# Weight loads ahead of the activations in one queue, and the first two chunks made block by block with plain products

## The chip, the cores and the metric

One core of one Trainium2 chip. The metric is the device time of one execution in microseconds (us). Each kernel ran several times. "Span" is the profiled execution seen from inside, some 2 us shorter than the device time of that same execution.

## The reference

x is fp32, 8 x 3008 x 256; the weights are float64, w_in 256 x 2048 and w_out 2048 x 256; the result is fp32.

```python
X = np.fft.fft(x, axis=1)
X = np.fft.fft(X, axis=2)
attn = X.real.astype(np.float32)                 # (8, 3008, 256)
h = attn.reshape(8 * 3008, 256) @ w_in           # inner dimension 2048
g = np.maximum(0.01 * h, h)
out = (g @ w_out).astype(np.float32)
```

## The kernel before

The transform along 256 is folded into w_in: a product of w_in with a small table gives `wf` ("fold"). The transform along 3008 is a product with sine and cosine tables ("dft"), made for 16 units (a batch element, even or odd frequencies). The result is worked off in 48 chunks of 2 x 251 or 2 x 250 columns, three to a unit, and for each chunk in 8 blocks `f` of the inner dimension: 384 steps. A step has an "up" (four products, VectorE's additions, ScalarE's leaky ReLU) and, three steps later, a "down" into w_out. VectorE's additions also use two rows: `wn`, a row of the folded weights, and `nb`, made from one column of x (`nyx`) by a transform of 8 rows ("nyquist"). Both go out to DRAM and come back in another layout. "Down" is a fast scheme with seven products in place of eight. It needs four sums of the activations in every step and four combinations of w_out's tiles; both are GpSimd's work.

```python
    def up(j, f):
        ...                                       # 4 products, then VectorE makes cos and g
        nc.scalar.activation(g, g, ACT.Lrelu)                                    # line 394
        a = [[g[:, r, h * n : (h + 1) * n] for h in range(2)] for r in range(2)]
        s = work.tile([P, 4, CW], F32, tag="s", bufs=4, name="s")
        s1, s2, s3, s4 = (s[:, i, 0:n] for i in range(4))
        nc.gpsimd.tensor_tensor(s1, a[1][0], a[1][1], op=ALU.add)
        nc.gpsimd.tensor_tensor(s2, s1, a[0][0], op=ALU.subtract)
        nc.gpsimd.tensor_tensor(s3, a[0][0], a[1][0], op=ALU.subtract)
        nc.gpsimd.tensor_tensor(s4, a[0][1], s2, op=ALU.subtract)
        hidden[j, f] = a[0][0], a[0][1], s4, a[1][1], s1, s2, s3

    turns = (0, 1, 5, 6, 4, 2, 3)

    def down(j, f):
        ...                                       # sums[j]: seven sums in four PSUM banks
        for i, p in enumerate(turns):             # seven products, line 416
            nc.tensor.matmul(sums[j][p], lhsT=still[p], rhs=moving[p], ...)
        ...                                       # after the last block: 7 additions, store
```

The weights arrive as float64 words. VectorE turns each 128x512 tile into fp32 with five instructions (and ScalarE with two): two on integers in `begin` (lines 247, 248), three in `end` (lines 260 to 262). There are 16 such tiles, eight of each weight. The head of the program:

```python
    w0 = load_w_in(0)                             # w_in, block 0: two tiles
    t0 = load_x(0, nc.scalar)                     # x: 2 x 1.5 MB on ScalarE's queue
    nc.scalar.dma_start(nyx, x_nyq)
    nc.sync.dma_start(feat_sb, ...)
    w2 = load_w_in(2 * WN)                        # w_in, block 2
    for n in range(4):
        load_tab(nc.sync, n, 0)                   # transform tables
    convert(w0)
    fold_w_in(0, w0)
    ...                                           # folds of x, then the transforms of unit 0
    convert(w2)
    fold_w_in(2 * WN, w2)
    spread_wn(0)()                                # the row wn goes through DRAM
    step(0)
    step(1)
    step(2)
    ...                                           # the other weights, one step between two of them
```

`step(at)` makes the "up" of step `at` and the "down" of step `at - 3`. The order written here is not binding inside an engine: the built program has its own fixed order, made by the scheduler.

Of the kernel before, what the change touches and what calls it, by code (L numbers as in the profile page):

```python
# [39 lines left out]
F32 = mybir.dt.float32  # L43
# [6 lines left out]
P = 128  # L50
# [7 lines left out]
CW = 251  # L58
NF = F // P
NH = NF // 2  # L60
WN = 512
WB = WN // D
# [88 lines left out]
def tile_fnet_leaky_relu(  # L151
# [24 lines left out]
    def load_x(b, q=None):  # L176
        t = xp.tile([P, 2, 2, NI * 2, D], F32, tag="x", bufs=1, name="xt")
        for h in range(2):
            (q or nc.sync).dma_start(t[:, h], x[b, :, h].rearrange("p e i r d -> p e (i r) d"))
        return t  # L180
# [3 lines left out]
    def fold_rows(t, h):  # L184


        a, z = t[:, h, 0], t[:, h, 1]
        nc.vector.tensor_tensor(a, a, z, op=ALU.add)  # L188
        lo, hi = a[:, :, 1:P], a[:, :, P + 1 : D]
        nc.vector.tensor_tensor(z[:, :, P + 1 : D], lo, hi, op=ALU.subtract)  # L190
        nc.vector.tensor_tensor(z[:, :, 1:P], lo, hi, op=ALU.add)
        nc.scalar.copy(z[:, :, 0:1], a[:, :, 0:1])
        nc.gpsimd.memset(z[:, :, P : P + 1], 0.0)
# [19 lines left out]
    def load_tab(q, n, c):  # L213
        t = const.tile([P, NI, KC], F32, name=f"tab_{n}_{c}")
        q.dma_start(t, seq_tab[n, c])
        tabs[n, c] = t
# [49 lines left out]
    def convert(made):  # L266
        for w in made:
            w.begin()
        for w in made:
            w.end()  # L270

    def load_w_in(f0):
        n, made = w_in.shape[1] // F, []
        for a in range(2):
            w = work.tile([P, WN], F32, tag="win", bufs=4, name="win")
            src = w_in[a * P : (a + 1) * P, n * f0 : n * (f0 + WN)].rearrange("p (c n) -> p c n", c=1)
            made.append(Weights(src, w))
        return made

    def fold_w_in(f0, made):  # L280

        for w in range(2):
            pt = up_ps()
            for a in range(2):
                nc.tensor.matmul(pt, lhsT=feat_sb[:, a, w * P : (w + 1) * P], rhs=made[a].dst, start=(a == 0), stop=(a == 1))  # L285
            nc.scalar.copy(wf[:, w, f0 : f0 + WN], pt)

    def spread_wn(f0):


        row = wn_dram[:, f0 : f0 + WN]
        nc.scalar.dma_start(row.rearrange("(o h) n -> o h n", o=1), wf[0:1, 1].rearrange("o (h n) -> o h n", h=2)[:, :, f0 : f0 + WN])
        at = f0 // P

        def rest():
            for h in range(2):
                nc.scalar.dma_start(wn[:, h * NH + at : h * NH + at + WN // P], row[h].rearrange("(q p) -> p q", p=P))
        return rest
# [9 lines left out]
    def combine_w_out(f):  # L308

        b = [[wo[:, h, f : f + WB, i * P : (i + 1) * P] for i in range(2)] for h in range(2)]  # L310
        t = [wt[:, i, f : f + WB, :] for i in range(4)]
        for to, x, y in ((t[0], b[0][1], b[0][0]), (t[1], b[1][1], t[0]), (t[2], b[1][1], b[0][1]), (t[3], b[1][0], t[1])):
            nc.gpsimd.tensor_tensor(to, x, y, op=ALU.subtract)
# [34 lines left out]
    def fold_nyquist():  # L348
        nc.vector.tensor_tensor(nyb, nya, nyb, op=ALU.add)
        nc.vector.tensor_tensor(nya[:, 0], nyb[:, 0], nyb[:, 1], op=ALU.add)  # L350
        nc.vector.tensor_tensor(nya[:, 1], nyb[:, 0], nyb[:, 1], op=ALU.subtract)
# [20 lines left out]
    mixed, spreads, hidden, sums = {}, {}, {}, {}  # L372
    units = [(b, c) for b in range(B) for c in range(2)]
    blocks, _ = chunks()
    steps = [(j, f) for j in range(len(blocks)) for f in range(NH)]

    def up(j, f):
        b, c, at, n, _ = blocks[j]
        pt = [up_ps("cos_ps"), up_ps("sin_ps")]
        for blk in range(2):  # L380
            for h in range(2):
                fs = slice((h * NH + f) * P, (h * NH + f + 1) * P)
                nc.tensor.matmul(pt[blk][:, h * n : (h + 1) * n], lhsT=wf[:, blk, fs],  # L383
                                 rhs=mixed[b, c][blk][:, at : at + n], start=True, stop=True)
        cos = work.tile([P, 2 * CW], F32, tag="cos", bufs=3, name="cos")
        for h in range(2):
            hs = slice(h * n, (h + 1) * n)
            nc.vector.scalar_tensor_tensor(cos[:, hs], in0=spreads[b, c][:, at : at + n],  # L388
                                           scalar=wn[:, h * NH + f : h * NH + f + 1],
                                           in1=pt[0][:, hs], op0=ALU.mult, op1=ALU.add)  # L390
        g = work.tile([P, 2 * WN], F32, tag="g", bufs=5, name="g")[:, 0 : 4 * n].rearrange("p (r k) -> p r k", r=2)
        nc.vector.tensor_tensor(g[:, 0], cos[:, 0 : 2 * n], pt[1][:, 0 : 2 * n], op=ALU.add)  # L392
        nc.vector.tensor_tensor(g[:, 1], cos[:, 0 : 2 * n], pt[1][:, 0 : 2 * n], op=ALU.subtract)  # L393
        nc.scalar.activation(g, g, ACT.Lrelu)  # L394
        a = [[g[:, r, h * n : (h + 1) * n] for h in range(2)] for r in range(2)]
        s = work.tile([P, 4, CW], F32, tag="s", bufs=4, name="s")
        s1, s2, s3, s4 = (s[:, i, 0:n] for i in range(4))
        nc.gpsimd.tensor_tensor(s1, a[1][0], a[1][1], op=ALU.add)  # L398
# [5 lines that stand above are left out]

    turns = (0, 1, 5, 6, 4, 2, 3)

    def down(j, f):
        _, _, _, n, first = blocks[j]
        if f == 0:
            banks = [ps.tile([P, 512], F32, tag="sum", bufs=4, name="sum_ps") for _ in range(4)]  # L410
            sums[j] = {p: banks[i // 2][:, 256 * (i % 2) : 256 * (i % 2) + n] for i, p in enumerate(turns)}
        moving = hidden.pop((j, f))
        still = (wo[:, 0, f, 0:P], wo[:, 1, f, 0:P], wo[:, 1, f, P:D], wt[:, 3, f], wt[:, 0, f], wt[:, 1, f], wt[:, 2, f])
        for i, p in enumerate(turns):

            nc.tensor.matmul(sums[j][p], lhsT=still[p], rhs=moving[p], start=(f == 0 and i % 2 == 0),  # L416
                             stop=(f == NH - 1), skip_group_check=True)
        if f < NH - 1:
            return
        p1, p2, p3, p4, p5, p6, p7 = (sums[j][p] for p in range(7))  # L420
        o = work.tile([P, 2 * WN], F32, tag="o", bufs=2, name="o")[:, 0 : 4 * CW].rearrange("p (a n) -> p a n", a=2)
        e = work.tile([P, 2 * WN], F32, tag="e", bufs=2, name="e")[:, 0 : 4 * CW].rearrange("p (a n) -> p a n", a=4)
        q1, u2, u3, v = (e[:, i, 0:n] for i in range(4))
        c11, c21, c12, c22 = (o[:, d, r * n : (r + 1) * n] for d in range(2) for r in range(2))
        nc.scalar.copy(q1, p1)
        for to, x, y in ((c11, q1, p2), (u2, q1, p6), (u3, u2, p7), (v, u2, p5), (c22, u3, p5), (c12, v, p3), (c21, u3, p4)):
            nc.vector.tensor_tensor(to, x, y, op=ALU.add)
        for d in range(2):
            nc.sync.dma_start(out[d * P : (d + 1) * P, first : first + 2 * n], o[:, d, 0 : 2 * n])

    lag = 3

# [24 lines left out]
    nc.vector.memset(inf[:, 0:1], 1151.0)  # L457
    nc.vector.memset(inf[:, 1:2], 255.0 * 2.0**23)
    w0 = load_w_in(0)
    t0 = load_x(0, nc.scalar)  # L460
    nc.scalar.dma_start(nyx, x_nyq)
    nc.sync.dma_start(feat_sb, feat_tab.rearrange("(a p) n -> p a n", p=P))
    w2 = load_w_in(2 * WN)
    for n in range(4):
        load_tab(nc.sync, n, 0)
    convert(w0)
    fold_w_in(0, w0)
    fold_rows(t0, 0)
    fold_rows(t0, 1)
    fold_halves(0, t0)  # L470
    fold_nyquist()
    nyquist(0)()
    dft(units[0], 0)()
    spread(units[0])
    dft(units[0], 1)()
    convert(w2)
    fold_w_in(2 * WN, w2)
    spread_wn(0)()
    step(0)
    step(1)  # L480
    step(2)
    o = load_w_out(0)
    convert(o)
    combine_w_out(0)
    w = load_w_in(WN)
    convert(w)
    fold_w_in(WN, w)
    step(3)
    w = load_w_in(3 * WN)
    for n in range(4):  # L490
        load_tab(nc.sync, n, 1)
    convert(w)
    fold_w_in(3 * WN, w)
    spread_wn(WN)()
    nyquist(1)()
    spread(units[1])
    for blk in range(2):
        dft(units[1], blk)()
    for f in range(WB, NH, WB):
        o = load_w_out(f)  # L500
        convert(o)
        combine_w_out(f)
        step(3 + f // 2)
    for at in range(7, len(steps) + lag):
        step(at)


# [28 lines left out]
```

## Time and profile before

| | before |
|---|---|
| device time, median of 6 runs | 1979.0 us (1978.8 to 1979.3) |
| span of the profiled run | 1977.1 us |
| TensorE busy | 1939.4 us |
| TensorE waiting | 33.2 us |
| first product starts | 23.0 us |
| first "up" starts | 44.5 us |

How to read it: span less busy less waiting leaves 4.5 us (nearly all of it behind the last product, which ends at 1972.6).

### The profile page before, as it was taken

The numbers are of one execution on the slowest core, as the hardware profiler recorded it, in microseconds if no ns is written. First come the engines' busy times: TensorE is split into PE (matmuls) and PEld (weight loads), VectorE is DVE, ScalarE is ACT, GpSimd is POOL, SyncE is SP. The second block draws the span as 40 slices with busy tenths as digits, with TensorE's granted clock in tenths as the row PEclk, the third lists the DMA queues.
The fourth block names the chain that finished last, engine by engine and source line by source line (L and its number), as shares of the span: only waits on it lengthen the run. The fifth ranks groups of instructions, "written<-read, shape, count | busy, mean of one in ns | idle before, by whom it ended". The sixth has DMA issues, their size and how long they took to land.

```text
span 1977.1 us, 24341 instructions
## 1 busy us (share of the span) xinstructions
PE 1939.4 (98%) x8888; PEld 1681.7 (85%) x8888; DVE 1103.0 (56%) x2089; ACT 460.7 (23%) x524; POOL 1092.1 (55%) x1572
## 2 busy tenths in 40 slices
PE   5899999999999999999999999999999999999999
PEld 2588888888888888888888888888888888888888
DVE  7965444574454745556554665447544474445444
ACT  3422222222222222222222222222222222222221
POOL 0675555565555655556555565556645565555554
PEclk9999999999999999999999999999999999999999
DMA  7300000020000100010000200002000020000000
GB/s 290 126 11 29 11 11 19 22 82 11 19 21 18 76 11 19 21 75 19 11 29 11 83 11 22 19 11 83 21 11 19 11 93 11 11 19 21 11 11 22
DMA packets 25598, 70.99 MB, mean 36 GB/s; under 512 B 4596, under 2 KB 17268, under 8 KB 23432
## 3 DMA queue, kind: packets, MB, share of 16 engines
q1 hardware_dynamic: 22928, 66.18, 9.3%
q10 hardware_dynamic: 2552, 3.26, 0.5%
q8 instruction: 71, 1.16, 0.2%
q14 instruction: 47, 0.39, 0.1%
HBM read 44.72 MB, written 24.71 MB: 35 GB/s over the span
## 4 chain that ended last, share of the span: by engine, by line
PE 96%; DVE 3%; DMA 1%; issue 0%; ACT 0%; ACTq 0%; DVEq 0%; SPq 0%
PE sum_ps L416 57%; PE sin_ps L383 16%; PE cos_ps L383 16%; PE dft_ps L318 6%; DMA raw<-in_w_in_dram 1%; DVE power L261 0%; PE up_ps L285 0%; DVE power L248 0%; DVE wo L260 0%; DVE wo L262 0%; DVE xt L188 0%; DVE wo L247 0%; DVE cos L388 0%; DMA wn<-wn_dram 0%; DVE win L260 0%
## 5 line engine op out<-in xcount | busy, mean ns | idle before, releaser
L388 DVE SCALAR_TENSOR_TENSOR cos<-nb,wn,cos_ps 128x251 f32<-128x251 f32 (+1 forms) x768 | 330.5, 472 | 725.4 <-PE cos_ps L383 724.4
L398 POOL TENSOR_TENSOR s<-g 128x251 f32<-128x251 f32 (+1 forms) x384 | 285.2, 743 | 797.1 <-ACT g L394 791.0
L394 ACT ACTIVATE g<-g 128x1004 f32<-128x1004 f32 (+1 forms) x384 | 399.1, 1039 | 1317.4 <-DVE g L393 1303.0
L416 PE MATMUL sum_ps<-s,wt 128*128 128x251 f32 (+1 forms) x2304 | 550.6, 374 | 0.0
L416 PEld LDWEIGHTS sum_ps<-s,wt 128*128 128x128 f32 x2304 | 434.1, 188 | 55.0
L383 PE MATMUL cos_ps<-mix,wf 128*128 128x251 f32 (+1 forms) x1536 | 388.8, 375 | 7.7 <-DVE cos L388 7.7
L383 PE MATMUL sin_ps<-mix,wf 128*128 128x251 f32 (+1 forms) x1536 | 388.5, 375 | 0.8 <-DVE mix L327 0.8
L416 PE MATMUL sum_ps<-g,wo 128*128 128x251 f32 (+1 forms) x1536 | 388.7, 375 | 0.0
L383 PEld LDWEIGHTS cos_ps<-mix,wf 128*128 128x128 f32 x1536 | 291.8, 190 | 43.0 <-DVE cos L388 8.1
L416 PEld LDWEIGHTS sum_ps<-g,wo 128*128 128x128 f32 x1536 | 291.8, 190 | 40.2
L383 PEld LDWEIGHTS sin_ps<-mix,wf 128*128 128x128 f32 x1536 | 290.7, 189 | 36.2 <-DVE mix L327 1.2
L399 POOL TENSOR_TENSOR s<-s,g 128x251 f32<-128x251 f32 (+1 forms) x384 | 294.0, 766 | 0.0
L401 POOL TENSOR_TENSOR s<-g,s 128x251 f32<-128x251 f32 (+1 forms) x384 | 276.4, 720 | 29.9
L392 DVE TENSOR_TENSOR g<-cos,sin_ps 128x502 f32<-128x502 f32 (+1 forms) x384 | 259.8, 676 | 49.6 <-DVE cos L388 11.2
L393 DVE TENSOR_TENSOR g<-cos,sin_ps 128x502 f32<-128x502 f32 (+1 forms) x384 | 257.1, 670 | 0.0
L400 POOL TENSOR_TENSOR s<-g 128x251 f32<-128x251 f32 (+1 forms) x384 | 255.2, 665 | 0.0
L416 PE MATMUL sum_ps<-g,wt 128*128 128x251 f32 (+1 forms) x768 | 225.2, 375 | 0.0
L416 PE MATMUL sum_ps<-s,wo 128*128 128x251 f32 (+1 forms) x768 | 225.2, 375 | 0.0
L416 PEld LDWEIGHTS sum_ps<-s,wo 128*128 128x128 f32 x768 | 145.5, 189 | 17.0
L416 PEld LDWEIGHTS sum_ps<-g,wt 128*128 128x128 f32 x768 | 145.9, 190 | 16.5
L318 PE MATMUL dft_ps<-tab,xt 128*128 128x377 f32 (+1 forms) x384 | 127.0, 480 | 1.7 <-DVE nyq L327 1.7
L318 PEld LDWEIGHTS dft_ps<-tab,xt 128*128 128x128 f32 x384 | 72.5, 189 | 45.8 <-DVE nyq L327 2.3
(43 smaller groups left out, 435.4 us busy)
## 6 DMA issues: line engine op xcount, KB each, us to landing
xt<-in_x_dram SPq DMA_DIRECT2D x14, 1536.0 KB, 10.0
out_dram<-o SPq DMA_DIRECT2D x80, 251.0 KB, 2.3
tab<-in_seq_tab_dram SPq DMA_DIRECT2D x8, 565.5 KB, 8.2
raw<-in_w_in_dram SPq DMA_DIRECT2D x8, 512.0 KB, 4.4
raw<-in_w_out_dram SPq DMA_DIRECT2D x8, 512.0 KB, 3.9
out_dram<-o SPq DMA_DIRECT2D x16, 250.0 KB, 2.4
xt<-in_x_dram ACTq DMA_DIRECT2D x2, 1536.0 KB, 10.0
nb<-nyq_dram SPq DMA_DIRECT2D x8, 376.5 KB, 4.1
```

The lines of the kernel that those rows point to most:

```text
L318: nc.tensor.matmul(ps_t[0:m, 0 : KW[c]], lhsT=z_of(i), rhs=tabs[n, c][:, i, 0 : KW[c]], start=(i == 0), stop=(i == NI - 1))
L383: nc.tensor.matmul(pt[blk][:, h * n : (h + 1) * n], lhsT=wf[:, blk, fs], rhs=mixed[b, c][blk][:, at : at + n], start=True, stop=True)
L388: nc.vector.scalar_tensor_tensor(cos[:, hs], in0=spreads[b, c][:, at : at + n], scalar=wn[:, h * NH + f : h * NH + f + 1], in1=pt[0][:, hs ...
L392: nc.vector.tensor_tensor(g[:, 0], cos[:, 0 : 2 * n], pt[1][:, 0 : 2 * n], op=ALU.add)
L393: nc.vector.tensor_tensor(g[:, 1], cos[:, 0 : 2 * n], pt[1][:, 0 : 2 * n], op=ALU.subtract)
L394: nc.scalar.activation(g, g, ACT.Lrelu)
L398: nc.gpsimd.tensor_tensor(s1, a[1][0], a[1][1], op=ALU.add)
L399: nc.gpsimd.tensor_tensor(s2, s1, a[0][0], op=ALU.subtract)
L400: nc.gpsimd.tensor_tensor(s3, a[0][0], a[1][0], op=ALU.subtract)
L401: nc.gpsimd.tensor_tensor(s4, a[0][1], s2, op=ALU.subtract)
L416: nc.tensor.matmul(sums[j][p], lhsT=still[p], rhs=moving[p], start=(f == 0 and i % 2 == 0), stop=(f == NH - 1), skip_group_check=True)
```

## The change

Its intent: w_in, needed first, is not to share the memory bandwidth with x (in `before`, between 2 and 12 us, x's queue moved 3.00 MB, in packets of 12,288 bytes, and w_in's 0.99 MB, in packets of at most 4,096); so all loads go into one queue in order of use, and both first w_in blocks are converted and folded before x is touched. Then VectorE, which has to convert the other twelve tiles during the first steps, is to be relieved: the first two chunks are made together, block by block, so that each pair of tiles serves two steps, and with eight plain products, which need neither GpSimd's sums nor the combined w_out.

```diff
-    steps = [(j, f) for j in range(len(blocks)) for f in range(NH)]
+    plain = 2
+    steps = [(j, f) for f in range(NH) for j in range(plain)]
+    steps += [(j, f) for j in range(plain, len(blocks)) for f in range(NH)]
 ...                                              # in up():
+        if j < plain:
+            hidden[j, f] = a
+            return
 ...
+    def down_plain(j, f):
+        ...                                       # two PSUM banks
+        for d in range(2):
+            for r in range(2):
+                for h in range(2):
+                    nc.tensor.matmul(sums[j][d][:, r * n : (r + 1) * n], lhsT=wo[:, h, f, d * P : (d + 1) * P], rhs=a[r][h], ...)
+        if f == NH - 1:                           # two ScalarE copies and the store
 ...                                              # the head:
     w0 = load_w_in(0)
-    t0 = load_x(0, nc.scalar)
-    nc.scalar.dma_start(nyx, x_nyq)
     nc.sync.dma_start(feat_sb, ...)
     w2 = load_w_in(2 * WN)
+    nc.sync.dma_start(nyx, x_nyq)
+    t0 = load_x(0)
     for n in range(4):
         load_tab(nc.sync, n, 0)
     convert(w0)
     fold_w_in(0, w0)
+    convert(w2)
+    fold_w_in(2 * WN, w2)
+    spread_wn(0)()
+    fold_nyquist()
     ...                                           # folds of x, then the transforms of unit 0
-    convert(w2)
-    fold_w_in(2 * WN, w2)
-    spread_wn(0)()
 ...                                              # then: one pair of weight tiles, two steps, in turn;
                                                  # unit 1's transforms come later, GpSimd's combinations last
```

More of the change, by code (lines that the diff above doesn't have):

```diff
@@ L405, in tile_fnet_leaky_relu, with put, out_tile @@
     turns = (0, 1, 5, 6, 4, 2, 3)
+    def put(o, n, first):
+        for d in range(2):
+            nc.sync.dma_start(out[d * P : (d + 1) * P, first : first + 2 * n], o[:, d, 0 : 2 * n])
+    def out_tile():
+        return work.tile([P, 2 * WN], F32, tag="o", bufs=2, name="o")[:, 0 : 4 * CW].rearrange("p (a n) -> p a n", a=2)
+    def down_plain(j, f):
+        _, _, _, n, first = blocks[j]
+        if f == 0:
+            sums[j] = [ps.tile([P, 512], F32, tag="sum", bufs=4, name="sum_ps") for _ in range(2)]
+        a = hidden.pop((j, f))
+        for d in range(2):
+            for r in range(2):
+                for h in range(2):
+                    nc.tensor.matmul(sums[j][d][:, r * n : (r + 1) * n], lhsT=wo[:, h, f, d * P : (d + 1) * P], rhs=a[r][h],
+                                     start=(f == 0 and r == 0 and h == 0), stop=(f == NH - 1 and h == 1), skip_group_check=True)
+        if f == NH - 1:
+            o = out_tile()
+            for d in range(2):
+                nc.scalar.copy(o[:, d, 0 : 2 * n], sums[j][d][:, 0 : 2 * n])
+            put(o, n, first)
     def down(j, f):
+        if j < plain:
+            down_plain(j, f)
+            return
         _, _, _, n, first = blocks[j]
@@ L420, in down @@
         p1, p2, p3, p4, p5, p6, p7 = (sums[j][p] for p in range(7))
-        o = work.tile([P, 2 * WN], F32, tag="o", bufs=2, name="o")[:, 0 : 4 * CW].rearrange("p (a n) -> p a n", a=2)
+        o = out_tile()
         e = work.tile([P, 2 * WN], F32, tag="e", bufs=2, name="e")[:, 0 : 4 * CW].rearrange("p (a n) -> p a n", a=4)
@@ L427, in down @@
             nc.vector.tensor_tensor(to, x, y, op=ALU.add)
-        for d in range(2):
-            nc.sync.dma_start(out[d * P : (d + 1) * P, first : first + 2 * n], o[:, d, 0 : 2 * n])
+        put(o, n, first)
     lag = 3
@@ L470, in tile_fnet_leaky_relu @@
     fold_halves(0, t0)
-    fold_nyquist()
     nyquist(0)()
@@ L475, in tile_fnet_leaky_relu, with some_steps @@
     dft(units[0], 1)()
-    convert(w2)
-    fold_w_in(2 * WN, w2)
-    spread_wn(0)()
-    step(0)
-    step(1)
-    step(2)
+    at = 0
+    def some_steps(n):
+        nonlocal at
+        for _ in range(n):
+            step(at)
+            at += 1
     o = load_w_out(0)
     convert(o)
-    combine_w_out(0)
+    some_steps(plain)
     w = load_w_in(WN)
@@ L487, in tile_fnet_leaky_relu @@
     fold_w_in(WN, w)
-    step(3)
+    some_steps(plain)
     w = load_w_in(3 * WN)
-    for n in range(4):
-        load_tab(nc.sync, n, 1)
     convert(w)
@@ L494, in tile_fnet_leaky_relu @@
     spread_wn(WN)()
+    some_steps(plain)
+    o = load_w_out(WB)
+    for n in range(4):
+        load_tab(nc.sync, n, 1)
+    convert(o)
+    some_steps(plain)
     nyquist(1)()
     spread(units[1])
-    for blk in range(2):
-        dft(units[1], blk)()
-    for f in range(WB, NH, WB):
+    for f in range(2 * WB, NH, WB):
         o = load_w_out(f)
         convert(o)
+        some_steps(plain)
+        dft(units[1], f // WB - 2)()
+    for f in range(0, NH, WB):
         combine_w_out(f)
-        step(3 + f // 2)
-    for at in range(7, len(steps) + lag):
-        step(at)
+    some_steps(len(steps) + lag - at)
 def kernel(x, moe_w_in, moe_w_out):
```

## The prediction

A difference of the ends of -13.9 us, taken as -13.5 after an allowance of about half a microsecond, gave 1979.0 - 13.5 = 1965.5 us.

> **What bounds the kernel now.** I read the page's first and fourth parts, then the waits of TensorE, then the timeline of TensorE and of VectorE over the first 110 us.
>
> ```profile
> PE 1939.4 (98%) x8888; PEld 1681.7 (85%) x8888; DVE 1103.0 (56%) x2089; ACT 460.7 (23%) x524; POOL 1092.1 (55%) x1572
> ...
> PE 96%; DVE 3%; DMA 1%; issue 0%; ACT 0%; ACTq 0%; DVEq 0%; SPq 0%
> ```
>
> TensorE is busy for 98% of a span of 1977.1 us and is 96% of the chain that ended last. Hardly anything but its own work and its idle time can move the end. All of its waits are these four:
>
> ```profile
> PE up_ps L285 <- DVE win L262: 23.0, 1, 23.0
> PE cos_ps L383 <- DVE cos L388: 7.7, 1, 7.7
> PE dft_ps L318 <- DVE nyq L327: 1.7, 1, 1.7
> PE sin_ps L383 <- DVE mix L327: 0.8, 1, 0.8
> ```
>
> That is 33.2 us, and the timeline puts every one of them before 86.3 us. From there to 1971.4 us TensorE never waits (busy 1884.2 of 1884.2 us between 87.2 and 1971.4). So the case is decided in the first 90 us. TensorE there:
>
> ```profile
> 23.00 6.47 PE L285 MATMUL up_ps<-win,feat_sb 128*128 128x512 f32 x8 [23.00 <-DVE win L262]
> 29.40 3.97 PE L318 MATMUL dft_ps<-tab,nyx 128*8 128x377 f32 x12
> 33.30 7.88 PE L318 MATMUL dft_ps<-tab,xt 128*128 128x377 f32 x24
> 41.02 3.60 PE L285 MATMUL up_ps<-win,feat_sb 128*128 128x512 f32 x8
> ...
> 55.76 2.04 PE L383 MATMUL cos_ps<-mix,wf 128*128 128x251 f32 x4 [7.75 <-DVE cos L388]
> ```
>
> The same eight instructions take 6.47 us when TensorE comes out of idleness and 3.60 us later: an idle spell costs about 3 us more than itself. The first 23 us are a chain, w_in arriving and VectorE converting it:
>
> ```profile
> 1.18 11.64 DMA raw<-in_w_in_dram
> 12.84 0.43 DVE win L247
> ```
>
> The second half of the first w_in block lands only at 12.84 us. The two 1.5 MB pieces of x on ScalarE's queue, issued at the same instant, land at about 8 and 13 us. After it VectorE is nearly full (8.6 to 10 of each 10 us from 20 us on): it takes in x, converts sixteen 128x512 weight tiles from float64 words (five instructions each) and makes the activations. The 7.75 us wait is for the row wn, which goes through DRAM and can start only when the second w_in block is folded, at 44 us.
>
> [...] while both queues are full, x moves about 3 MB in the time in which w_in moves 1 MB, the packets being 12,288 and 4,096 bytes, so x in its own queue holds back what is needed first. [...] full clock comes some 5.5 us after the first matmul, is lost in the 7.75 us wait (mean granted clock 0.66 between 50 and 60 us), and returns at about 59 us. [...] the 128x512 tensor_scalar of line 248 takes 0.42 us with GpSimd idle and up to 0.95 us with it busy. [...] a 251-column product, two records here, takes 0.424.
>
> **The change part by part: extra products.** In steady state a step is 4.67 us: 1.70 for four "up" products (8 records x 0.212 us) and 2.97 for the seven of the fast scheme (14 records). The plain form has eight: 16 x 0.212 = 3.40. Sixteen steps (two chunks, eight blocks) pay 0.425 each: +6.8 us of TensorE, all on the path. GpSimd loses 64 sums, VectorE fourteen additions; neither is on the path.
>
> **Head loads.** The queue carries, in order, w0 (1.05 MB), feat (0.26), w2 (1.05), nyx (0.10), x (3.15), four tables (2.32), two w_out tiles (1.05). Before, some 4.3 MB had come by 12.84 us and 390 to 430 GB/s flowed after. I take a landing as 2.8 us + MB/0.42: first w_in tiles at 4.1 and 5.3, w2 at 7.2 and 8.4, x at 12.4 and 16.1, tables from 17.5 to 21.6, w_out at 22.9 and 24.1 us.
>
> **The head, on the built order of each engine.** VectorE's spacings without GpSimd are 0.34 us for a tensor_scalar, 0.60 for each scalar_tensor_tensor (2.5 us a tile), 1.67 + 0.86 + 0.86 for half of x, 3.3 for the last two folds of x. The order now is w0, w2, x. w0 is converted at about 10 us (ScalarE's first table load, 1.28 us, delays it a little); TensorE starts at 9.7 in place of 23.0. w2 is done at 15, x's folds at 18.5, 21.9, 23.6 and 25.2. TensorE: fold w0, cold, to about 16; fold w2 to 19.7; the 8-row transform, as soon as two tables are in, to 23.6; the two transforms of the first unit to 31.6. So the first step begins at about 31.6 instead of 44.5 with both w_in blocks already folded. wn is back by about 27. The row nb: its butterfly waits for x's last fold, 26.1 us; before, nb landed 6.1 us after its butterfly, so about 32.3, just when VectorE is free for it (33.6). The 7.75 us wait goes.
>
> **The catch-up.** VectorE must still convert the four tiles of w_in blocks 1 and 3 among the first steps. Following the built order: TensorE waits about 1 us for the second transform's butterfly, 1.5 us for the first activation (at 37.2), 1.3 us for the last w_in tile of block 1 (42.8), 2.3 us for that of block 3 (52.4), and makes the sixth "up" by 60.5 us. After that two plain steps plus their pair of tiles cost VectorE 4 + 5 = 9 us, against 2 x 5.09 = 10.2 of TensorE, and GpSimd, with no sums to make, no longer slows it. I expect no further wait: the combinations (16 GpSimd operations) have four steps' time, and the four sum banks are freed by four ScalarE copies while TensorE does the next "up".
>
> **The sum.** Before, at 87.2 us, five "ups", one "down" and all transforms of unit 1 are done. After, at 60.5 us: six "ups" and two plain "downs", but the three transforms of unit 1 (36 records x 0.32 = 11.5 us) still ahead. Difference of the ends: 60.5 - 87.2 - 1.70 (one more "up") - 2.97 (one more "down") + 14 x 0.425 (plain steps still ahead) + 11.5 = -13.9 us. The check by idle time: before 33.2 us idle and about 5 of cold clock; after 9.7 + 6 idle and 3 cold; 38 - 19 - 6.8 = 12. With half a microsecond for what I overlooked: 1979.0 - 13.5 = 1965.5 us.
>
> **The rivals.** First, the weights bound VectorE however the steps are arranged, so the idle time moves into the first six steps. For it: VectorE is nearly full from 12.8 to 92 us before, and by my count is still full to 64 us after. Against it: some 30 us of its time was spent at rates slowed by GpSimd, now idle there. If the stalls came to 11 us instead of 6, the time is about 1971. Second, the single queue turns against the change: x and the tables arrive last, and w_in block 1 stands behind the write of the 8-row transform, which waits for VectorE. For it: any load behind that write is held until 26 us. Against: tables have 1 to 5 us of slack and block 1 is wanted only at 38. If the queue ran 15% slower the head would come 2 to 3 us later, about 1968. Third, the plain products eat the gain: if only the earlier start were kept and the middle wait returned in another form (nb in place of wn), 13 - 6.8 leave 6, about 1973. The nb chain has little slack in my timeline (1 us), so I give this some weight. In the other direction: if the stalls of the catch-up vanish (tiles converted earlier than I reckon) the time is about 1960.
>
> **Range and chances.** The central case is 1965.5; the rivals stand at 1968 to 1973, the good case at 1960. Stalls I have not seen are likelier than ones I invented, so the range leans up: 1961 to 1971. Two per cent is 39.6 us: more than all idle time there is (33.2), and the extra products are 6.8 against a saving that would have to turn into a loss of 33. So within 2% is as good as certain: 0.98, with 0.01 on either side.
>
> **What would show it.** First matmul near 9.7 us, first "cos" near 31.6 us, and no wait of TensorE over 3 us between the first step and 90 us; waits of TensorE summing to about 16 us in place of 33.2; line 429's products 256 x 2 records at 0.212 us apart; no wait after 65 us, and none where the third chunk takes the sum banks. VectorE's 128x512 conversions should stay near 0.42 and 0.69 us throughout. It is wrong if w_in's second half lands after 8 us, if TensorE waits on nb or on a w_out tile for more than 3 us, if the clock drops again after 31 us, or if the period of a later step differs from 4.67 us.

## The result, and the profile after

| | before | after |
|---|---|---|
| device time, median of 6 runs | 1979.0 us | 1964.85 us (1964.4 to 1966.2) |
| span of the profiled run | 1977.1 us | 1964.4 us |
| TensorE busy | 1939.4 us | 1945.9 us |
| TensorE waiting | 33.2 us | 14.0 us |
| first product / first "up" | 23.0 / 44.5 us | 10.24 / 32.65 us |

The ratio is 0.9929 (0.9917 to 0.9942), so within 2%. A ratio here and below is the mean time of one kernel's fast runs over the mean of the other's of the same rounds, so not quite the ratio of the medians. The outputs of the changed kernel, and of every experiment, agreed with the reference.

The page of the changed kernel, busy time by engine and the chain that ended last:

```profile
PE 1945.9 (99%) x8920; PEld 1687.8 (86%) x8920; DVE 1090.4 (56%) x2075; ACT 462.4 (24%) x526; POOL 1036.1 (53%) x1508
...
PE 98%; DVE 1%; DMA 1%; ACT 0%; SPq 0%; issue 0%; DVEq 0%
```

TensorE has 6.5 us more to do, and 32 records (16 products, two records each) more. VectorE and GpSimd have less. All waits of TensorE (us in total, times, longest):

```profile
PE up_ps L286 <- DVE win L263: 10.2, 1, 10.2
PE sum_ps L429 <- ACT g L397: 2.0, 1, 2.0
PE dft_ps L319 <- DVE xt L199: 1.0, 1, 1.0
PE sin_ps L386 <- DVE mix L327: 0.8, 1, 0.8
```

19.2 us of waiting have gone and 6.5 us of work have come: 12.7, the difference of the two spans. (The medians differ by 14.15: the profiled run of the changed kernel took 1966.17 us, the longest of the six; see the two kinds of runs below.) The wait for w_in has shrunk from 23.0 to 10.2 us and the middle wait of 7.7 us, for wn, is no more. TensorE's timeline (start, length, line, operation, count, idle time before and its releaser):

```profile
10.24 9.75 PE L286 MATMUL up_ps<-win,feat_sb 128*128 128x512 f32 x16 [10.24 <-DVE win L263]
19.92 3.98 PE L319 MATMUL dft_ps<-tab,nyx 128*8 128x377 f32 x12
24.93 7.88 PE L319 MATMUL dft_ps<-tab,xt 128*128 128x377 f32 x24 [1.03 <-DVE xt L199]
32.65 1.01 PE L386 MATMUL cos_ps<-mix,wf 128*128 128x251 f32 x4
...
39.26 6.20 PE L429 MATMUL sum_ps<-g,wo 128*128 128x251 f32 x20 [1.99 <-ACT g L397]
45.30 3.60 PE L286 MATMUL up_ps<-win,feat_sb 128*128 128x512 f32 x8
```

Both folds (x16) now stand in front of the transforms. Look at 39.26: twenty records took 6.20 us, where 0.212 us each would make 4.24. The windows view of that stretch has the cause (length, then the busy time of PE, PEld, DVE, ACT and POOL, then the granted clock, the DMA share and GB/s):

```profile
39.26:45.30 6.04, 6.04 (x21) 5.11 (x21) 6.04 (x14) 3.82 (x6) 0.00 (x0) 0.72 1.01 392
```

The clock was 0.72 on average: after the idle spell of 2.0 us the clock record has one stretch of 3.41 us at 0.5. Last, VectorE's timeline at the start (same columns as TensorE's):

```profile
4.68 0.43 DVE L248 TENSOR_SCALAR win<-raw 128x512 int32<-128x512 int32 x1 [3.79 <-DMA raw<-in_w_in_dram]
...
5.98 0.43 DVE L248 TENSOR_SCALAR win<-raw 128x512 int32<-128x512 int32 x1
...
7.95 0.43 DVE L248 TENSOR_SCALAR win<-raw 128x512 int32<-128x512 int32 x1 [0.61 <-DMA raw<-in_w_in_dram]
```

Line 248 begins a tile: w0's two tiles are begun at 4.68 and, without a wait for it, at 5.98 us, w2's first at 7.95. Before, w0's second tile could be begun only at 12.84. (In the built order w2's first tile comes ahead of the last four instructions on w0, so VectorE waited 0.6 us for w2 before it finished w0.)

The changed kernel has two kinds of runs. In those with a mean clock of 1.000 it takes 1964.4 to 1965.1 us, in those with 0.999 it takes 1966.2 to 1966.6, about 1.6 us more. Of the six runs above one was of the latter kind, the profiled one; of five later ones (`after_again`) four were. The stretch of 3.41 us at half clock costs 1.7 us (an estimate, half of its length), so it is likely what separates the kinds; no run with a clock of 1.000 was profiled. Differences under 2 us are therefore read below within one kind, or not at all.

### The profile page after: what moved, and what is told of

Its sections match the earlier page's. It is cut to its first block, busy times and chain, and to the rows that moved or that the text cites. A ratio compares the mean times of both kernels' runs of the same rounds, so it can differ in the third digit from the quotient of the medians.

```text
span 1964.4 us, 24292 instructions
## 1 busy us (share of the span) xinstructions
PE 1945.9 (99%) x8920; PEld 1687.8 (86%) x8920; DVE 1090.4 (56%) x2075; ACT 462.4 (24%) x526; POOL 1036.1 (53%) x1508
## 4 chain that ended last, share of the span: by engine, by line
PE 98%; DVE 1%; DMA 1%; ACT 0%; SPq 0%; issue 0%; DVEq 0%
PE sum_ps L449 56%; PE cos_ps L386 16%; PE sin_ps L386 16%; PE dft_ps L319 6%; PE sum_ps L429 3%; DMA raw<-in_w_in_dram 1%; PE up_ps L286 0%; DVE xt L189 0%; DVE power L262 0%; DVE win L263 0%; DVE xt L191 0%; DVE xt L200 0%; DVE xt L192 0%; DMA nyq_dram<-nyq 0%; ACT power L250 0%
## 5 line engine op out<-in xcount | busy, mean ns | idle before, releaser
L404 POOL TENSOR_TENSOR s<-g 128x251 f32<-128x251 f32 (+1 forms) x368 | 271.7, 738 | 781.2 <-ACT g L397 781.2
L449 PE MATMUL sum_ps<-s,wt 128*128 128x251 f32 (+1 forms) x2208 | 527.6, 374 | 0.0
L449 PEld LDWEIGHTS sum_ps<-s,wt 128*128 128x128 f32 x2208 | 416.1, 188 | 52.6
L449 PE MATMUL sum_ps<-g,wo 128*128 128x251 f32 (+1 forms) x1472 | 372.5, 375 | 0.0
L449 PEld LDWEIGHTS sum_ps<-g,wo 128*128 128x128 f32 x1472 | 279.6, 190 | 38.7
L405 POOL TENSOR_TENSOR s<-s,g 128x251 f32<-128x251 f32 (+1 forms) x368 | 277.7, 755 | 0.0
L407 POOL TENSOR_TENSOR s<-g,s 128x251 f32<-128x251 f32 (+1 forms) x368 | 262.6, 714 | 28.6
L406 POOL TENSOR_TENSOR s<-g 128x251 f32<-128x251 f32 (+1 forms) x368 | 241.6, 657 | 0.0
L449 PE MATMUL sum_ps<-g,wt 128*128 128x251 f32 (+1 forms) x736 | 215.8, 375 | 0.0
L449 PE MATMUL sum_ps<-s,wo 128*128 128x251 f32 (+1 forms) x736 | 215.8, 375 | 0.0
L449 PEld LDWEIGHTS sum_ps<-g,wt 128*128 128x128 f32 x736 | 139.8, 190 | 15.8
```

What stands on the lines that cost most here:

```text
L449: nc.tensor.matmul(sums[j][p], lhsT=still[p], rhs=moving[p], start=(f == 0 and i % 2 == 0), stop=(f == NH - 1), skip_group_check=True)
```

## The experiments

My theory was that of the prediction: the earlier first product and the vanished wn wait make the gain; the plan of the first two chunks keeps the catch-up of the conversions short; the plain products cost 6.8 us. The rivals: the head alone does it all; or the plan does nothing but cost; or GpSimd's silence is the essential part. Runs stood beside runs of the kernel before on the same chip (medians 1979.1 to 1979.3).

### The new head alone

The kernel before with the head of the diff; chunks one by one, with the fast scheme throughout.

```diff
 before, and: x and nyx in the same queue behind w2; convert and fold w2,
 spread wn, fold nyx before the folds of x
```

> The kernel before with the new head alone (loads in one queue, both w_in blocks folded before x); chunks one by one, fast products. My theory: the first step begins at 32.7 us as in the changed kernel, but VectorE, full from 12 to 92 us before, cannot convert twelve more tiles beside GpSimd's sums any faster, so most of the 12 us gained comes back as waits of TensorE on converted tiles between 40 and 85 us: 1970 to 1973 us, waits of TensorE 22 to 28 us. Rival (the head is the whole gain, the interleaving buys nothing and its products cost 6.8 us): 1957 to 1960 us, waits about 14 us, faster than the changed kernel.

Measured: 1966.37 us, ratio 0.9936 (0.9921 to 0.995); busy 1941.9, waiting 18.7. Its longest waits:

```profile
PE up_ps L285 <- DVE win L262: 15.3, 4, 10.8
PE sum_ps L416 <- POOL s L399: 1.4, 2, 1.1
```

12.75 us come with the head alone (1979.12, its neighbours' median, less 1966.37). Both expectations missed: the catch-up costs only 4.5 us on w_in tiles and 1.4 on sums, not the 10 or more that I had reckoned from VectorE being full, but it isn't free either. Against `head_only` the whole plan of the first two chunks is worth 1.5 us by the first median of the changed kernel (1964.85), and nothing by the second (1966.3, `after_again` below): what it saves in waits (18.7 us to 14.0) it adds to TensorE's work (1941.9 to 1945.9).

### The new plan with the old queues

```diff
     w0 = load_w_in(0)
+    t0 = load_x(0, nc.scalar)
+    nc.scalar.dma_start(nyx, x_nyq)
     nc.sync.dma_start(feat_sb, ...)
     w2 = load_w_in(2 * WN)
-    nc.sync.dma_start(nyx, x_nyq)
-    t0 = load_x(0)
```

> The changed kernel with x and the Nyquist column back on ScalarE's queue, everything else as changed. Theory: w_in's second half lands near 13 us again (7 us later than now), the first product moves from 10.2 to about 18 us; some of it is hidden because the head is bound by VectorE's folds of x, so the end moves by 3 to 6 us: 1968 to 1971 us. Rival (the queue order hardly matters, the plan of the first chunks does all): within 1 us of the changed kernel.

Measured: 1975.23 us, ratio 0.998 (0.9965 to 0.9994): 10.4 us above the changed kernel by the medians, 9.6 to 9.7 within one kind of run. The expectation (1968 to 1971) missed. The chain of its head (start, length):

```profile
1.17 11.80 DMA raw<-in_w_in_dram
12.97 0.02 issue
12.99 0.43 DVE win L248
13.42 0.34 DVE power L249
13.76 0.60 DVE win L261
14.36 1.67 DVE xt L189
...
19.66 1.67 DVE xt L189
21.33 1.20 DVE power L262 x2
22.54 1.20 DVE win L263 x2
```

This is w0's second tile: it is begun at 12.99 us in place of 5.98, 7.0 later. I had counted on little more than that, less what is won back behind it. But from there to the first product it is now 10.2 us instead of 4.3: in the built order VectorE takes in x (line 189 and its like, 1.67 + 0.86 + 0.86 + 1.67 = 5.1 us) and starts on w2 ahead of the end of w0's conversion. The second queue costs 7.0 us of landing and, with the order that the scheduler makes for it, 5.9 more on VectorE. The first product starts at 23.19, as before the change. A part of the delay is won back behind it, where other waits disappear.

The parts don't add up: head alone 12.75, everything but the queue (so the new plan and the new order of the folds) 3.9, all together 14.15. They shorten in part the same idle time.

### One queue, x ahead of w_in

```diff
+    t0 = load_x(0)
+    nc.sync.dma_start(nyx, x_nyq)
     w0 = load_w_in(0)
     ...
-    nc.sync.dma_start(nyx, x_nyq)
-    t0 = load_x(0)
```

> The changed kernel with one load queue still, but x and the Nyquist column ahead of w_in in it. Theory (it is the order of arrival that counts, not the number of queues): w_in lands at about 12 to 13 us, as with two queues, VectorE takes x first, the first product comes at 20 to 23 us and the end at 1972 to 1976 us. Rival (sharing between two queues is the loss, one queue is good in any order): 1964 to 1968 us.

Measured: 1969.71 us, ratio 0.9952 (0.9937 to 0.9967): 4.9 us above the changed kernel, between the two expectations; the first product starts at 17.63 us. So the order within the queue is worth 4.9 us. The rest of the 10.4 (5.5 by the medians, 4.7 to 4.8 within one kind) comes only with the second queue: x's halves are begun by VectorE at 7.2 and 10.9 us here, and w0, begun at 13.62, is not waited for. How much of this rest is the shared bandwidth and how much VectorE's other order is not separated.

### Plain products, chunk by chunk

```diff
-    steps = [(j, f) for f in range(NH) for j in range(plain)]
-    steps += [(j, f) for j in range(plain, len(blocks)) for f in range(NH)]
+    steps = [(j, f) for j in range(len(blocks)) for f in range(NH)]
 and one step, not two, between two weights
```

> New head and plain products for the first two chunks, but chunk by chunk, not block by block. Theory: what matters is that TensorE has two steps of work per pair of converted tiles; without it TensorE waits on tiles as in the run of the head alone, less because GpSimd is idle (conversions at 0.42 and 0.69 us), and the extra products still cost 6.8 us: 1969 to 1975 us. Rival (freeing GpSimd is what speeds the catch-up): waits as in the changed kernel, about 14 us, and 1965 us.

Measured: 1967.19 us, ratio 0.9939 (0.9922 to 0.9955); waiting 16.1. Interleaving, with the order of loads and of unit 1's transforms that goes with it, is worth 2.3 us by the medians and between runs with a clock of 1.000, 1.1 between those with 0.999: more than the nothing of the rival, less than I thought.

### The plain chunks with GpSimd's sums made all the same

```diff
-        if j < plain:
-            hidden[j, f] = a
-            return
         s = work.tile([P, 4, CW], F32, tag="s", bufs=4, name="s")
         ...                                       # the four sums
+        if j < plain:
+            hidden[j, f] = a
+            return
```

The 64 sums are made and not used; nothing waits for them.

> The changed kernel, but GpSimd still makes the 64 sums of the first two chunks, which nobody reads. Theory (TensorE has slack of work for VectorE once the chunks are interleaved): VectorE's conversions slow by some 30 per cent between 40 and 75 us, TensorE waits 1 to 4 us more: 1966 to 1969 us. Rival (GpSimd's absence is essential): 1971 us or more; rival (no matter at all): 1965 us.

Measured: 1972.15 us, ratio 0.9965 (0.995 to 0.998): 7.3 us above the changed kernel by the medians, 5.4 between runs with a clock of 0.999. Here the rival that calls GpSimd's absence essential was right. VectorE's conversions of w_out tiles between 26 and 90 us (busy us, mean ns of one; then idle before), first in the changed kernel:

```profile
L261 DVE SCALAR_TENSOR_TENSOR wo<-raw,wo 128x512 f32<-128x512 uint32 x8 | 6.4, 815 | 0.0
L263 DVE SCALAR_TENSOR_TENSOR wo<-wo,power 128x512 f32<-128x512 f32 x8 | 5.3, 681 | 0.0
L248 DVE TENSOR_SCALAR wo<-raw 128x512 int32<-128x512 int32 x8 | 3.3, 417 | 0.0
```

and with the unused sums:

```profile
L261 DVE SCALAR_TENSOR_TENSOR wo<-raw,wo 128x512 f32<-128x512 uint32 x8 | 8.3, 1042 | 0.0
L263 DVE SCALAR_TENSOR_TENSOR wo<-wo,power 128x512 f32<-128x512 f32 x8 | 7.0, 900 | 0.0
L248 DVE TENSOR_SCALAR wo<-raw 128x512 int32<-128x512 int32 x8 | 5.4, 681 | 0.0
```

The same instructions, 28 to 63% longer, beside a busy GpSimd. TensorE gets a wait of 3.8 us for a transform's butterfly (the sum and difference of its two halves, lines 327 and 328) that stands behind them on VectorE. So what the plain products give is not in the products (they cost), but in GpSimd's silence: it is worth 5.4 to 7.3 us here, and the products cost 6.8. That the two nearly cancel agrees with `head_only`, which has neither and takes about the same time as the changed kernel. The trace also has a GpSimd sum of 7.75 us where its like take about 0.7; see below.

### Two more plain chunks

```diff
+    plain_too = (0, 1, 24, 25)                    # chunks 24 and 25, far from the head
```

> The changed kernel with chunks 24 and 25 (in the middle, where TensorE never waits) also made with plain products, one after the other. Theory: a plain step costs TensorE one product of 0.425 us more and nothing else: 16 x 0.425 = +6.8 us, 1971.6 us, no new wait. Rival (plain steps give something back even in steady state, by freeing GpSimd, or lose something at the sum banks): off that by more than 1 us.

Measured: 1972.27 us, ratio 0.9963 (0.9947 to 0.998). Within one kind of run the difference from the changed kernel is 6.7 us (clock 1.000) and 6.9 us (0.999). 6.8 for two plain chunks is confirmed.

### The clock kept up from the start

```diff
+    idle = const.tile([P, WN], F32, name="idle")
+    nc.gpsimd.memset(idle, 0.0)
+    pt = up_ps("idle_ps")
+    for _ in range(6):
+        nc.tensor.matmul(pt, lhsT=idle[:, 0:P], rhs=idle, start=True, stop=True)
```

> The changed kernel with six 128x512 products of zeros, read by nobody, at the start, so that TensorE is at full clock when w_in comes. Theory: the eight products of the folds take about 6.9 us in place of 9.75, but the transform of the first unit waits for VectorE's last fold of x at 24.9 us in any case, so the end does not move: within 1 us of 1964.9, the wait on the fold of x growing from 1.0 to about 4 us. Rival (the cold start costs its full 3 us): 1962 us.

Measured: 1966.53 us, ratio 0.9936 (0.9921 to 0.995). The two folds ran warm (3.70 us each, where together they took 9.75) and each was finished earlier, but the tiles and x came no sooner: TensorE waited 1.9 us for x's fold, and in this run the transform behind it took 9.57 us in place of 7.88, which I read as a lowered clock. All four runs were of the 0.999 kind, and against the changed kernel's runs of that kind there is no difference. That transform began at 25.13 us, in the changed kernel at 24.93: the cold start is hidden behind VectorE's folds of x. The wait did not grow to 4 us as expected, since w2 came no sooner; and the drop of the clock was, by this reading, not avoided but moved, from the first plain products (twenty records in 4.53 us here, in 6.20 there) to this transform.

### Unit 1's transforms moved into the gap

If TensorE waits for w_in tiles in `head_only`, other work could stand there: the transforms of unit 1, which need only tables and x.

```diff
 head_only, and: unit 1's four tables loaded, and its three transforms made,
 right after the first w_out tiles instead of after w_in block 3
```

> The run of the head alone, with fast products for all chunks one by one, and the second unit's transforms (11.5 us of TensorE that need only 3 us of VectorE) moved to where TensorE waited there for w_in blocks 1 and 3. Theory now (after the first four runs: with the new head what is left to gain in the catch-up is some 9 us of waits and cold clock, and the plain products pay 6.8 for 8): the waits on w_in tiles between 47 and 58 us vanish, 1958 to 1963 us, faster than the changed kernel. Rival (VectorE is the bound to 85 us whatever TensorE does): the waits move to w_out tiles after 65 us, 1965 to 1968 us.

Measured: 1965.88 us, ratio 0.9932 (0.9917 to 0.9946), no different from `head_only` within the spread; the expected 1958 to 1963 missed. The waits on w_in tiles after the first did vanish, but another took their place:

```profile
PE up_ps L285 <- DVE win L262: 10.0, 1, 10.0
PE sum_ps L416 <- POOL wt L313: 5.6, 1, 5.6
```

TensorE waits for a combination of w_out on GpSimd, and GpSimd's own timeline says why (start, length):

```profile
60.94 10.73 POOL L398 TENSOR_TENSOR s<-g 128x251 f32<-128x251 f32 x1 [5.79 <-ACT g L394]
71.64 0.62 POOL L400 TENSOR_TENSOR s<-g 128x251 f32<-128x251 f32 x1
72.22 1.16 POOL L399 TENSOR_TENSOR s<-s,g 128x251 f32<-128x251 f32 x1
```

One sum of 128x251 took 10.73 us; its like take about 0.7. VectorE in that time (first and last instructions of an unbroken run):

```profile
60.65 0.75 DVE L247 TENSOR_SCALAR wo<-raw 128x512 int32<-128x512 int32 x2
61.32 0.68 DVE L260 SCALAR_TENSOR_TENSOR wo<-raw,wo 128x512 f32<-128x512 uint32 x1
...
70.41 0.69 DVE L262 SCALAR_TENSOR_TENSOR wo<-wo,power 128x512 f32<-128x512 f32 x1
71.01 0.86 DVE L388 SCALAR_TENSOR_TENSOR cos<-nb,wn,cos_ps 128x251 f32<-128x251 f32 x2
```

From 60.65 to 71.0 us VectorE runs one instruction after another whose inputs lie in SBUF (the memory of the tiles), at its full speed (0.68 us, not slowed), and GpSimd's sum ends just after VectorE has turned to an instruction with an input in PSUM (where the products arrive). So the sum lasted as long as a row of some twenty VectorE instructions. Two others were long beside an unbroken row of conversions: 4.52 us at 44.93 in this trace, 7.75 at 40.26 in `dead_sums`. That the row keeps GpSimd out is my reading; by what means, no trace here shows.

### Gaps in VectorE's row of conversions

```diff
 dft_early, and in Weights.end, after each of the three instructions:
+            v.memset(self.raw[:, 0:1], 0.0)       # likewise raw[:, 1:2], power[:, 0:1]
```

One-column writes, so that VectorE's instructions with SBUF inputs don't follow one another directly.

> The run with early transforms (all chunks fast), with a one-column VectorE memset after each of the last three instructions of a conversion, so that VectorE's stream of SBUF operations is broken up by writes that read nothing. The scheduler also reorders a little, so the length of single GpSimd operations before 90 us is the sign, not the time alone. Theory (GpSimd gets in only where VectorE's stream has a gap): no GpSimd operation of 251 columns over 3 us, in place of 4.5 and 10.7; the 5.6 us wait shrinks to under 2, 1959 to 1963 us. Rival (a gap of one small instruction does not let it in, only an operation on PSUM or idle time does): operations of 5 us and more stay, 1965 to 1968 us.

Measured: 1963.9 us, ratio 0.9921 (0.9904 to 0.9937). The sum that had taken 10.73 us:

```profile
62.77 0.71 POOL L401 TENSOR_TENSOR s<-g 128x251 f32<-128x251 f32 x1 [6.83 <-ACT g L397]
```

The longest GpSimd instruction of that stretch was 3.61 us; I had expected none over 3. The time, too, was 0.9 us above what I expected: the built order had changed and other waits had come (2.2 us for a w_out tile, 1.8 for a w_in tile). So this supports the reading that GpSimd is kept out by VectorE's unbroken row, and doesn't prove it alone: the instructions around the sum are not the same as before.

### One plain chunk

If GpSimd's silence is what is bought, one plain chunk is enough, since a chunk has eight blocks and takes all 16 tiles. First `plain_by_chunk` with `plain = 1`, beside a repeat of the changed kernel:

> The run with plain products chunk by chunk, but only the first chunk plain. Theory: the second chunk's plain products bought nothing there (by its first step VectorE has nearly done converting), so eight products of 0.425 us go: 3.4 us less than the run with two, 1963.8 us. Rival (GpSimd, set to work 40 us earlier, is held off by VectorE and holds TensorE up): 1966 us or more.

> The changed kernel unaltered, on the same chip and in the same rounds as the two candidates beside it. Expected: 1964.9 us within half a microsecond; rounds whose granted clock is 1.000 some 1.5 us shorter than those with 0.999.

Measured: one_plain_late 1963.91 us, ratio 0.9922 (0.9909 to 0.9936), 3.3 below `plain_by_chunk`, about the 3.4 of one chunk's plain products, with the same 16.1 us of waiting. The changed kernel again: 1966.3 us (1964.6 to 1966.6), ratio 0.9933 (0.992 to 0.9945), its median in the other kind of run this time, so above the 1964.9 expected.

Then the same with unit 1's transforms in the gap, as in `dft_early`:

```diff
-    plain = 2
+    plain = 1
 chunk by chunk; unit 1's tables and transforms right after the first w_out tiles
```

> Only the first chunk plain, chunk by chunk, and the second unit's transforms moved forward as in the run with early transforms. Theory: there the only new wait, 5.6 us on GpSimd's combined weights, came from one GpSimd sum that took 10.7 us while VectorE converted back to back; with the first chunk plain GpSimd has no sums in that stretch, the wait goes, 3.4 us of products come in: 1960 to 1962 us, faster than the changed kernel by 3 to 5 us. Rival (the wait was for VectorE's conversion of the w_out tiles themselves): the wait stays, 1966 us or more.

Measured: 1959.64 us (1959.4 to 1961.2), ratio 0.9902 (0.9889 to 0.9916); busy 1940.0. All its waits:

```profile
PE up_ps L286 <- DVE win L263: 10.3, 1, 10.3
PE dft_ps L319 <- DVE xt L199: 1.8, 1, 1.8
PE sin_ps L385 <- DVE mix L327: 0.8, 1, 0.8
PE sin_ps L385 <- DVE g L395: 0.4, 1, 0.4
```

This is the best version, a little better than expected: 6.0 us below the changed kernel by the means of the same rounds (1959.95 and 1965.98), some 5 below its runs with a clock of 1.000, which all four runs here have. There is no wait after the first few "ups", and no idle spell of 2.0 us: the transforms fill it. One GpSimd instruction was long here as well, a combination of 7.74 us where its like take about 0.7, at a time when nothing needed it; what VectorE did beside it was not asked.

## Why the prediction was right

The time (1965.5 predicted, 1964.85 measured) and the range held. By its steps:

- **What bounds it, and the sum.** Right. The difference of the ends was predicted as -13.9 us before an allowance of half a microsecond; measured -14.15.
- **Landings and the first product.** The first three w_in tiles were predicted at 4.1, 5.3 and 7.2 us and begun by VectorE at 4.68, 5.98 and 7.95, so 0.6 to 0.8 us later; "wrong if w_in's second half lands after 8 us" did not come about. The first product came at 10.24 instead of 9.7, the first "up" at 32.65 instead of 31.6, the sixth "up" ended at 61.5 instead of 60.5. Each is 0.5 to 1 us late, none changes the argument. (ScalarE's table load, named as a delay, ran from 0.74 to 2.02 us and delayed nothing; VectorE's wait for w2 ahead of the end of w0 is a delay that was not named.) What the prediction had of x's queue was only the bandwidth; that VectorE's order is nearly as large a part of the 23 us (5.9 us beside 7.0) is shown by `two_queues`.
- **The wn wait goes, nb doesn't replace it.** Right: neither stands in the list of waits. The reading of the old wait was incomplete, though: `wn` was written out at 45.61, but read back only at 50.74 on ScalarE's queue, behind a ScalarE instruction that had waited 2.4 us for VectorE's conversions (`before`, ScalarE's timeline); the reading itself took 3.08 us. So not only the way through DRAM was long.
- **Plain products, +6.8 us.** Right: `two_more_plain` 6.7 and 6.9. (The prediction calls line 429's work 256 x 2 records; it is 128 products, 256 records. The sum used the right number.)
- **Catch-up waits, about 6 us besides the first.** The sum of all waits was 14.0 for about 16, but by other items. The waits of 1.3 and 2.3 us for the last tiles of w_in blocks 1 and 3 did not come, a wait of 1.0 us on x's fold had not been counted, and the wait for the first activation was 2.0 instead of 1.5. In place of the two missing waits the first plain products ran cold, some 2 us longer (6.20 for 4.24). In the profiled run that hid a wait: the last tile of block 1 was finished at 44.65 us, TensorE came to it at 45.30, and at full clock would have come at some 43.5 (an estimate, 39.26 + 4.24). So there two errors cancelled, which is luck. Whether they do in the other kind of run is open: those are 1.6 us shorter, so hardly a wait can have taken the place of the cold stretch there, and none was profiled.
- **"Wrong if the clock drops again after 31 us."** It did drop in the profiled run, and by the mean clock in 5 of 11 runs. The criterion was too strict: by the difference of the two kinds it is worth 1.6 us. The idle spell before it was 2.0 us; after an equal one in `dead_sums` the clock stayed at 1.00 (40 to 60 us), so its length alone doesn't decide it.
- **Conversions at 0.42 and 0.69 us throughout.** Right for most; w_out tiles beside which GpSimd's combinations run take longer (one instruction of 1.12 us at 32.83, and over all eight tiles line 261's mean is 815 ns). `dead_sums` shows that this step carried more than I gave it: without GpSimd's silence the time is 1972, outside the range.
- **The rivals.** The first, the weights binding VectorE however the steps stand, fell in the changed kernel and came true in `dead_sums`, where GpSimd works beside plain products (in `head_only`, where it works beside fast ones, the time is 1966.4). The second, the one queue turning against the change, fell: there is no such wait. The third, that the plain products eat the gain, was half right in a way that it didn't put: nearly the whole gain (12.75 of 14.15; by the later median of the changed kernel, all of it) is there without them, and one plain chunk instead of two, with work moved into the gap, is better by 6.0 us.

What stays open: how the loss with two queues divides between bandwidth and VectorE's order; why the built order of VectorE puts x's folds into w0's conversion in `two_queues` (the scheduler's reasons are in no trace), and whether a long GpSimd instruction can be ended by any short break in VectorE's row.

## What to carry to other kernels

Where a kernel is bound by one engine to 98%, look for its idle time in the head: put what the first product needs alone at the front of the load queue (the new head alone gave 12.75 us here), and look also at whether the engine that prepares it has been given other work between its pieces (5.9 us in `two_queues`). Count what a relief costs on the bound engine: plain products (3.4 us a chunk) paid here only as long as GpSimd, silenced by them, would have slowed the conversions (28 to 63% longer beside it in `dead_sums`), that is for one chunk, not two (`one_plain_late` is 3.3 us below `plain_by_chunk`). Parts of a change that shorten the same idle time don't add (12.75 and 3.9 us came to 14.15); measure each alone before keeping both.
